# Attention and routed MoE on one core: z and v of the next batch split in another block, by another engine

## The chip, the cores and the metric

The kernel runs on one core of one Trainium2 chip. The metric is the device time of one execution in microseconds (us); the median of the runs is compared. PE is TensorE, DVE is VectorE, ACT is ScalarE, POOL is GpSimd, SP is SyncE, which issues most of the DMAs.

## What is computed

The reference, cut to its core: attention without softmax, a dense MLP, then a routed one.

```python
B, S, D = u.shape                      # 8, 3072, 256;  z is 8 x 3072 x 64
scores = np.matmul(z, z.transpose(0, 2, 1)) / S
attn = np.maximum(scores, 0.0) ** 2
x = (u * np.matmul(attn, v)).reshape(B * S, D)
h = x @ w_in                           # 256 x 2048
x = (h * np.clip(h + 3.0, 0.0, 6.0) / 6.0) @ w_out
e_idx = np.argmax(x @ w_gate, axis=1)  # 8 experts, the best one for each token
out = gate * sigmoid(x @ w_output_gate) * (relu(x @ w1[e]) @ w2[e])
```

## The kernel before

**Precision by splitting.** Each operand of a matmul is held as a high part (rounded by a cast to the matmul's type) and a low part (the operand less its high part), and three products take the place of one. So every tile of z and of v is split when it arrives: a cast on ACT gives the high part and a subtraction gives the low one.

**Blocks.** A batch has 6 chunks of 512 tokens, 48 chunks in all. `order` (lines 132 to 142) is a list of units written out in advance. A block ("A", q) has 24 attention units, a block ("M", q) has 16 units of the dense MLP, and ("E", t, p) are the experts' units at the end. From the third M block on, A and M take turns: A(q), then M(q - 1), then A(q + 1). The M block between the last A block of one batch and the first A block of the next is called the M block between two batches here. There are 7 of them, and 7 last A blocks whose batch has a next one.

**One step.** `run` (lines 747 to 759) goes through the units. In step n it issues the front of unit n + 3 (`stage1`: the matmuls into one of two PSUM banks "psa", then the activation on ACT and, in an M unit, `gt` on DVE, line 232, which frees the bank), the middle of unit n + 2 (`stage2`: the split into `hit` and `lot`), and the products of unit n (`back`). All other work is hung on a step by `when(step, fn)`. Its instructions stand in their engines' queues behind those of step - 1 and in front of those of the step named. Each engine takes its queue in order, since `manual_schedule` keeps the order of issue.

**What an engine does in one unit.** In an A unit ACT makes two activations (lines 220 and 221) and DVE a cast (line 240) and a subtraction (line 243). In an M unit ACT makes line 231 and the cast of line 242, DVE lines 232 and 243. Beside the units of an A block DVE also makes 32 products for the routing of an earlier chunk (`gate_dot`, line 431). The routing's small instructions (`route`, lines 373 to 411) follow in the last steps of the A block and the first of the M block, with the product with u (`mul_x`, line 277) and the scatter of rows from POOL's queue (line 420).

**z and v of the next batch.** `plan_chunk` (lines 683 to 689) hangs them on the last A block of a batch, whose first unit is s0. `load_z` (two DMAs on SP's queue) and `prep_z1` run for 6 tiles of z, `load_v` (one DMA) and `prep_v` for 12 pairs of v tiles. `prep_z1` (lines 159 to 176) makes two casts on ACT and one subtraction, for the first tile of a batch two. `prep_v` (lines 190 to 196) makes one cast on ACT and one subtraction. For every batch but the first the subtractions of z are POOL's (line 172); those of v always are (line 195). Raw tiles have two buffers each ("zraw" and "vraw"), so a third load waits until a first one was split. The high and low parts of v have 12 buffers (`NV`), as many as a batch needs, and the split z has 7.

Of the kernel before, what the change touches and what calls it, by code (L numbers as in the profile page):

```python
# [8 lines left out]
F32 = mybir.dt.float32  # L9
# [10 lines left out]
P = 128  # L20
# [7 lines left out]
def kernel(  # L28
# [14 lines left out]
    DQ = zT.shape[1]  # L43
# [24 lines left out]
    pe, act, dve, pool, sp = nc.tensor, nc.scalar, nc.vector, nc.gpsimd, nc.sync  # L68
# [76 lines left out]
    def when(step, fn, early=False):  # L145
        bg.setdefault((max(step, low[0]), not early), []).append(fn)

# [1 line left out]
    z1, z2, zraw = {}, {}, {}  # L149
    vh, vl, vraw = {}, {}, {}  # L150
    xu = {}
# [1 line left out]
    def load_z(key, b, t):  # L153
        zr = ap.tile([P, TC], F32, tag="zraw", name="zr", bufs=2)
        for h in range(2):
            sp.dma_start(out=zr[h * DQ:(h + 1) * DQ], in_=zT[b, :, t * TC:(t + 1) * TC])
        zraw[key] = zr

    def prep_z1(key, b, t, with_z2=False):
        zr = zraw.pop(key)  # L160
        a = ap.tile([P, TC], F32R, tag="z1", name="z1t", bufs=NZ + 1)
        if with_z2:
            w = ap.tile([P, TC], F32R, tag="z2", name="z2t", bufs=2)
            z2[b, t] = w
        else:
            w = ap.tile([P, TC], F32R, tag="zs", name="zst", bufs=1)
        act.copy(a[0:DQ], zr[0:DQ])
        if b or t:
            act.copy(w[DQ:P], zr[DQ:P])
        else:  # L170
            dve.tensor_copy(w[DQ:P], zr[DQ:P])
        eng = pool if b else dve
        eng.tensor_sub(a[DQ:P], zr[DQ:P], w[DQ:P].bitcast(F32))
        if with_z2:
            eng.tensor_sub(w[0:DQ], zr[0:DQ], a[0:DQ].bitcast(F32))
        z1[b, t] = a

    def prep_z2(key, b, t):
        zr = zraw.pop(key)
        w = ap.tile([P, TC], F32R, tag="z2", name="z2t", bufs=2)  # L180
        act.copy(w[DQ:P], zr[DQ:P])
        dve.tensor_sub(w[0:DQ], zr[0:DQ], z1[b, t][0:DQ].bitcast(F32))
        z2[b, t] = w

    def load_v(b, i):
        r = ap.tile([P, 2, D], F32, tag="vraw", name="vr", bufs=2)
        sp.dma_start(out=r, in_=v[b, 2 * i * P:2 * (i + 1) * P, :].rearrange("(a p) d -> p a d", p=P))
        vraw[b, i] = r

    def prep_v(b, i):  # L190
        r = vraw.pop((b, i))
        h = ap.tile([P, 2, D], F32R, tag="vh", name="vht", bufs=NV)
        l = ap.tile([P, 2, D], F32R, tag="vl", name="vlt", bufs=NV)
        act.copy(h, r)
        pool.tensor_sub(l, r, h.bitcast(F32))
        vh[b, i], vl[b, i] = h, l

    def load_u(q):
        b, c = divmod(q, NC)
        t = mp.tile([P, ND, TC], F32, tag="xu", name="xut", bufs=2)  # L200
        sp.dma_start(out=t, in_=uT[b, :, c * TC:(c + 1) * TC].rearrange("(d p) t -> p d t", p=P))
        xu[q] = t

# [1 line left out]
    tmp_t, hi_t, lo_t, o_t = {}, {}, {}, {}  # L205
    xh, xl = {}, {}

# [64 lines left out]
                mm(o[s], gh, wo[:, i].rearrange("p k d -> p (k d)"), i == 0, False)  # L272
                mm(o[s][:, :D], gl, wo[:, i, 0, :], False, i == NF - 1)

# [1 line left out]
    def mul_x(q, d):  # L276
        dve.tensor_mul(xu[q][:, d, :], xu[q][:, d, :], o_t[q][d][:, :TC])

    def split_x(q, d):
        if q in alt:  # L280
            if d == 0:
                alt[q] = pools["e"].tile([P, 2, ND, TC], F32R, tag="ws", name="xat", bufs=NPAIR + 2)
            h, l = (alt[q][:, k, d, :] for k in range(2))
        else:
            h = mp.tile([P, TC], F32R, tag="xph", name="xht", bufs=ND)
            l = mp.tile([P, TC], F32R, tag="xpl", name="xlt", bufs=ND)
        act.copy(h, xu[q][:, d, :])
        xh.setdefault(q, []).append(h)
        xl.setdefault(q, []).append(l)

    def split_xl(q, d):
        pool.tensor_sub(xl[q][d], xu[q][:, d, :], xh[q][d].bitcast(F32))

    def save_x(q):
        sp.dma_start(out=xsave[q], in_=xu.pop(q).rearrange("p d t -> p (d t)"))

    def reload_x(q):
        t = mp.tile([P, ND, TC], F32, tag="xu", name="xut", bufs=2)
        sp.dma_start(out=t, in_=xsave[q].rearrange("p (d t) -> p d t", d=ND))
        xu[q] = t  # L300

    alt = {NQ - 1: None, 1: None}

# [1 line left out]
    raw = {}  # L305

    def load_w(which, f):
# [45 lines left out]
        pool.tensor_sub(mf, mf, h.bitcast(F32))  # L353
        pool.tensor_add(l, mf, sc)

# [1 line left out]
    rt = {}  # L357

    def rtile(name, shape, dt=F32):
# [53 lines left out]
    def evacuate(q, s):  # L413
        o, row = o_t["x", q], row_of(q)
        act.activation(row[:, s, :D], o[s][:, :D], AF.Copy, scale=1.0 / 6.0)
        dve.scalar_tensor_tensor(row[:, s, :D], o[s][:, D:], 1.0 / 6.0, row[:, s, :D],  # L416
                                 op0=ALU.mult, op1=ALU.add)

    def scatter(q, s):
        pool.indirect_dma_start(  # L420
            out=xs_d,
            out_offset=bass.IndirectOffsetOnAxis(ap=rt["di", q][:, s:s + 1], axis=0),
            in_=row_of(q)[:, s, :],
            in_offset=None,
        )

    def gate_dot(q, k):
        s, e = divmod(k, E)
        if k == 0:
            rt["lg"] = rtile("lg", [P, NSUB, E])  # L430
        dve.tensor_tensor_reduce(junk, row_of(q)[:, s, :D], gbc[:, e, :], 1.0, 0.0, op0=ALU.mult, op1=ALU.add,  # L431
                                 accum_out=rt["lg"][:, s, e:e + 1])

# [1 line left out]
    small = {}  # L435

    def stile(name, w=E):
# [72 lines left out]
                           min_val=e * REG, max_val=e * REG + NT)  # L510
        sp.dma_start(out=xs_d[bass.ds(r, SLOT), :].rearrange("(a p) c -> p a c", p=P), in_=zrow)

# [1 line left out]
    rows, wraw, wreg, wnew, ws, ogw, gt = {}, {}, {}, {}, {}, {}, {}  # L514
    y_ps = []

# [122 lines left out]
        pools["row"] = pools["e"].tile([P, NSUB, RW], F32, name="row1")  # L639
        pool.memset(pools["row"][:, :, D + 2:RW], 0.0)  # L640

# [1 line left out]
    def plan_chunk(q):  # L643
        b, c = divmod(q, NC)
        s0, e0 = at["A", q, 0], at["A", q, NJ - 1]
        m0, m1 = at["M", q, 0], at["M", q, NF - 1]
        if q > 1:
            when(s0 + 4, lambda: load_u(q))
        if c > 0:
            when(s0 - 14, lambda: load_z(("2", q), b, c))  # L650
            when(s0 - 8, lambda: prep_z2(("2", q), b, c))
        for d in range(ND):
            when(e0 + 1 + 2 * d, lambda d=d: mul_x(q, d))
        if q < NSAVE:
            when(e0 + 5, lambda: save_x(q))
            when(m0 - NF - 8, lambda: reload_x(q))
        sx = m0 - NF + 4 if q < NSAVE or q == NQ - 1 else m0 - NJ + 2
        for d in range(ND):
            when(sx + 2 * d, lambda d=d: split_x(q, d))
            when(sx + 2 * d + 1, lambda d=d: split_xl(q, d))  # L660
        kind = order[m1 + 1][0]
        rate = {"A": 1.6, "M": 3.0 if q else 1.0, "E": 0.5}[kind]
        d0 = m1 + 2 if kind != "E" else m1 + 22
        for k in range(NSUB * E):
            when(d0 + int(k / rate), lambda k=k: gate_dot(q, k))
        n = d0 + int(NSUB * E / rate)
        for s in range(NSUB):
            when(m1 + 1 + (s if kind == "A" else 0), lambda s=s: evacuate(q, s))
        for st in range(1, 5):
            when(n + st - (st == 1), lambda st=st: route(q, st))  # L670
        sc = m1 + NJ + 2 if kind == "A" else n + 4
        if q < NSAVE:
            E0 = at["E", 0, 0]
            sc = max(E0 + 1, sc + (E0 + 1 - sc) % NPAIR)
        for st in range(NSUB):
            when(sc + (st * NPAIR if q < NSAVE else 0), lambda st=st: scatter(q, st))
        if q == 1:
            for st in range(4):
                when(n + 6 + st, lambda st=st: table2a(st))
            when(n + 11, lambda: tableb(1))  # L680
            for e in range(E):
                when(sc + NPAIR * (NSUB + e), lambda e=e: fill_tail(e))
        if c == NC - 1 and b + 1 < B:
            for t in range(NZ):
                when(s0 + 4 * t - 2, lambda t=t: load_z(("1", b + 1, t), b + 1, t))
                when(s0 + 4 * t + 2, lambda t=t: prep_z1(("1", b + 1, t), b + 1, t, t == 0))
            for i in range(NV):
                when(s0 + 2 * i - 2, lambda i=i: load_v(b + 1, i))
                when(s0 + 2 * i + 2, lambda i=i: prep_v(b + 1, i))

    for q in range(NQ):
        plan_chunk(q)
# [28 lines left out]
    load_v(0, 0)  # L721
    setup_consts()
    prep_z1(("1", 0, 0), 0, 0, True)
    prep_v(0, 0)
    load_z(("1", 0, 1), 0, 1)
    load_v(0, 1)
# [13 lines left out]
    front = {"A": stage1, "M": stage1, "E": e1}  # L740
    middle = {"A": stage2, "M": stage2, "E": lambda u: None}
    behind = {"A": back, "M": back, "E": e3}
# [68 lines left out]
```

## Time and profile before

| what | us |
|---|---|
| median of 3 runs | 5626.42 (5626.34 to 5627.16) |
| span of the profiled execution, first to last instruction | 5624.6 |
| what lies around that span, against the median | 1.8 |
| PE busy | 5533.8 (98%) |
| DVE busy | 4356.8 (77%) |
| ACT busy | 3446.1 (61%) |
| POOL busy | 1084.1 (19%) |

The page gives the profiled execution by its span; its own time outside the span is not listed, so the median stands in for it. Busy shares are means over stages, so this profile is read block by block: the start of a block is the start of its first matmul into "psa". In a timeline a row has the start, the duration and the instruction, with the idle time before it and what ended that in brackets. A group of instructions has count, busy time and mean duration, and behind the second bar the idle time in front of them. In a table of windows each engine has its busy time and, in brackets, its instructions, then the granted clock of PE as a share of 2.4 GHz, the DMA engines' busy share and GB/s.

### The profile page before, as it was taken

Reading aid. Unit: us, or ns where it says so; the run is one execution under the profiler, and the core shown is the slowest. Engines: PE = TensorE matmul, PEld = TensorE weight load, DVE = VectorE, ACT = ScalarE, POOL = GpSimd, SP = SyncE. Lnnn points to the kernel's source line nnn. Section 1 sums busy time; section 2 is a strip of 40 time slices with the busy share of each in tenths; the row PEclk is TensorE's granted clock in tenths of the full one; section 3 lists DMA queues with packets and bytes.
Section 4 is the critical chain, followed back from the end, with each engine's and each line's share of the span. In section 5 each row is a group of like instructions: output and inputs, shape, how many; then the busy total and the mean of one; then the engine's idle time right before and its main releaser. Section 6 shows DMA issues by size and latency. Waiting matters only on the chain.

```text
span 5624.6 us, 83062 instructions
## 1 busy us (share of the span) xinstructions
PE 5533.8 (98%) x28472; PEld 4644.1 (83%) x28472; DVE 4356.8 (77%) x9925; ACT 3446.1 (61%) x5870; POOL 1084.1 (19%) x915
## 2 busy tenths in 40 slices
PE   9999999999999999999999999999999999999999
PEld 6778887888788878887888788878888899999998
DVE  9877777767776777777776877686767888888887
ACT  7655565656565565556565656565555577777776
POOL 3220002000200020002000200020001144444443
PEclk9999999999999999999999999999999999999999
DMA  3110001000100010001000100010000122222243
GB/s 103 42 45 17 14 16 46 16 14 16 46 16 14 18 44 18 18 14 47 14 16 16 46 14 16 16 46 14 16 16 12 50 75 82 81 72 73 76 116 114
DMA packets 133151, 216.92 MB, mean 39 GB/s; under 512 B 16605, under 2 KB 85982, under 8 KB 132576
## 3 DMA queue, kind: packets, MB, share of 16 engines
q1 hardware_dynamic: 113888, 160.66, 9.9%
q0 software_dynamic: 18816, 50.75, 2.5%
q8 instruction: 225, 3.69, 0.3%
q14 instruction: 222, 1.82, 0.1%
HBM read 157.17 MB, written 55.22 MB: 38 GB/s over the span
## 4 chain that ended last, share of the span: by engine, by line
PE 88%; DVE 7%; issue 3%; ACT 1%; POOL 1%; DMA 0%; POOLq 0%; SPq 0%; ACTq 0%; DVEq 0%
PE psa L209 36%; PE psx L209 28%; PE pso L209 24%; DVE lot L243 2%; DVE hit L240 2%; DVE junk L431 1%; PE pso L574 1%; POOL out L625 0%; DVE wst L567 0%; ACT at L220 0%; DVE lot L597 0%; DVE r_cnt L394 0%; DVE cvt L323 0%; ACT gt L231 0%; DVE row L416 0%
## 5 line engine op out<-in xcount | busy, mean ns | idle before, releaser
L231 ACT ACTIVATE gt<-psa,three 128x512 f32<-128x512 f32 x768 | 528.8, 689 | 1147.4 <-PE psa L209 1076.2
L232 DVE SCALAR_TENSOR_TENSOR gt<-gt,psa 128x512 f32<-128x512 f32 x768 | 527.8, 687 | 878.2 <-ACT gt L231 877.9
L209 PE MATMUL psx<-wo,hit 128*128 128x512 f32 x3072 | 1112.5, 396 | 0.0
L209 PE MATMUL psa<-xht,win 128*128 128x512 f32 x2944 | 1039.5, 393 | 3.0 <-DVE gt L232 2.9
L220 ACT ACTIVATE at<-psa 128x512 f32<-128x512 f32 x1152 | 687.5, 597 | 552.9 <-PE psa L209 416.4
L243 DVE TENSOR_TENSOR lot<-at,hit 128x512 fp32r<-128x512 f32 x1152 | 882.9, 766 | 49.4 <-DVE hit L240 0.5
L209 PE MATMUL pso<-lot,vht 128*128 128x512 f32 x2208 | 891.7, 404 | 27.1 <-DVE lot L243 26.6
L209 PE MATMUL pso<-hit,vht 128*128 128x512 f32 x2208 | 883.3, 400 | 34.2 <-DVE hit L240 34.2
L209 PE MATMUL pso<-hit,vlt 128*128 128x512 f32 x2208 | 878.3, 398 | 0.0
L209 PE MATMUL psx<-wo,lot 128*128 128x256 f32 x3072 | 860.3, 280 | 0.0
L221 ACT ACTIVATE at<-at 128x512 f32<-128x512 f32 x1152 | 729.1, 633 | 36.7
L431 DVE CUSTOM_DVE_ANT_0 junk<-row,gbc 128x256 f32<-128x256 f32 x1536 | 714.2, 465 | 19.7
L209 PEld LDWEIGHTS psx<-wo,hit 128*128 128x128 f32 x3072 | 577.0, 188 | 136.2
L209 PEld LDWEIGHTS psa<-xht,win 128*128 128x128 f32 x2944 | 552.9, 188 | 134.5 <-DVE gt L232 5.6
L209 PE MATMUL psa<-xht,wst 128*128 128x256 f32 x3200 | 649.3, 284 | 1.9 <-DVE wst L567 1.3
L209 PEld LDWEIGHTS psx<-wo,lot 128*128 128x128 f32 x3072 | 579.6, 189 | 30.6
L243 DVE TENSOR_TENSOR lot<-gt,hit 128x512 fp32r<-128x512 f32 x768 | 527.6, 687 | 73.1 <-ACT hit L242 73.1
L209 PE MATMUL psa<-xlt,win 128*128 128x512 f32 x1472 | 580.1, 394 | 0.0
L209 PE MATMUL psx<-wst,hit 128*128 128x512 f32 x1600 | 577.1, 394 | 0.0
L567 DVE TENSOR_TENSOR wst<-w,wst 128x1024 fp32r<-128x1024 f32 x400 | 572.2, 1431 | 0.0
L240 DVE CAST hit<-at 128x512 fp32r<-128x512 f32 x1152 | 566.8, 492 | 2.4 <-ACT at L221 2.2
L420 POOL DMA_INDIRECT xs_d<-row,r_di x192 | 189.6, 988 | 1929.5 <-DVE row L411 1634.3
(154 smaller groups left out, 9251.5 us busy)
## 6 DMA issues: line engine op xcount, KB each, us to landing
w<-in_wcat SPq DMA_DIRECT2D x64, 512.0 KB
x<-xs_d SPq DMA_DIRECT2D x100, 260.0 KB
vr<-in_v SPq DMA_DIRECT2D x96, 256.0 KB
xut<-in_uT SPq DMA_DIRECT2D x48, 512.0 KB
zr<-in_zT SPq DMA_DIRECT2D x176, 128.0 KB
ogt<-in_w_ogT SPq DMA_DIRECT2D x100, 128.0 KB
wraw<-in_w_in SPq DMA_DIRECT2D x16, 256.0 KB
wraw<-in_w_out SPq DMA_DIRECT2D x16, 256.0 KB
```

The costliest lines, as they stand in the source:

```text
L209: pe.matmul(o, l, r, start=start, stop=stop)
L220: act.activation(t, ps, AF.Relu, scale=1.0 / S)
L221: act.activation(t, t, AF.Square)
L231: act.activation(t, ps, AF.Relu, bias=three)
L232: dve.scalar_tensor_tensor(t, t, 6.0, ps, op0=ALU.min, op1=ALU.mult)
L240: dve.tensor_copy(h, t)
L243: dve.tensor_sub(l, t, h.bitcast(F32))
L420: pool.indirect_dma_start(out=xs_d, out_offset=bass.IndirectOffsetOnAxis(ap=rt["di", q][:, s:s + 1], axis=0), in_=row_of(q)[:, s, :], in_o ...
L431: dve.tensor_tensor_reduce(junk, row_of(q)[:, s, :D], gbc[:, e, :], 1.0, 0.0, op0=ALU.mult, op1=ALU.add, accum_out=rt["lg"][:, s, e:e + 1])
L567: dve.tensor_sub(w[:, :, 1, :], wraw[p], w[:, :, 0, :].bitcast(F32))
L574: pe.transpose(o[:, d, a * P:(a + 1) * P], x[:, a, d * P:(d + 1) * P], ident)
```

## The change

All subtractions of z and v for batches after the first go to DVE, and the steps they are hung on move behind e0, the last unit of the last A block. The changed lines that only remove comments are left out.

```diff
-        eng = pool if b else dve
-        eng.tensor_sub(a[DQ:P], zr[DQ:P], w[DQ:P].bitcast(F32))
+        dve.tensor_sub(a[DQ:P], zr[DQ:P], w[DQ:P].bitcast(F32))
         if with_z2:
-            eng.tensor_sub(w[0:DQ], zr[0:DQ], a[0:DQ].bitcast(F32))
+            dve.tensor_sub(w[0:DQ], zr[0:DQ], a[0:DQ].bitcast(F32))
...
         act.copy(h, r)
-        pool.tensor_sub(l, r, h.bitcast(F32))
+        (dve if b else pool).tensor_sub(l, r, h.bitcast(F32))
...
         if c == NC - 1 and b + 1 < B:
             for t in range(NZ):
-                when(s0 + 4 * t - 2, lambda t=t: load_z(("1", b + 1, t), b + 1, t))
-                when(s0 + 4 * t + 2, lambda t=t: prep_z1(("1", b + 1, t), b + 1, t, t == 0))
+                at_z = e0 + 1 + (5 * t) // 2
+                when(at_z - 4, lambda t=t: load_z(("1", b + 1, t), b + 1, t))
+                when(at_z, lambda t=t: prep_z1(("1", b + 1, t), b + 1, t, t == 0))
             for i in range(NV):
-                when(s0 + 2 * i - 2, lambda i=i: load_v(b + 1, i))
-                when(s0 + 2 * i + 2, lambda i=i: prep_v(b + 1, i))
+                at_v = e0 + 2 + (6 * i) // 5
+                when(at_v - 3, lambda i=i: load_v(b + 1, i))
+                when(at_v, lambda i=i: prep_v(b + 1, i))
```

The M block between two batches has the units e0 + 1 to e0 + 16. The splits of z stand at steps e0 + 1, 3, 6, 8, 11 and 13, those of v at e0 + 2, 3, 4, 5, 6, 8, 9, 10, 11, 12, 14 and 15.

## Rows read from the trace of the kernel before

**Rows 1.** The page, part 1: busy time of each engine

```profile
PE 5533.8 (98%) x28472; PEld 4644.1 (83%) x28472; DVE 4356.8 (77%) x9925; ACT 3446.1 (61%) x5870; POOL 1084.1 (19%) x915
```

**Rows 2.** Windows of the 7 last A blocks: first, last, sum

```profile
339.84:398.70 58.86, 48.75 (x200) 36.76 (x199) 55.22 (x113) 42.37 (x75) 26.60 (x18) 0.97 0.23 70
...
3648.63:3706.85 58.22, 51.07 (x201) 38.88 (x200) 54.60 (x112) 42.35 (x75) 26.31 (x18) 0.91 0.21 64
sum 408.80, PE 348.91 PEld 265.21 DVE 383.41 ACT 296.78 POOL 184.67; mean PE 49.84 PEld 37.89 DVE 54.77 ACT 42.40 POOL 26.38
```

**Rows 3.** Windows of an M block and an A block inside a batch

```profile
488.42:533.10 44.68, 44.68 (x222) 37.26 (x221) 24.61 (x52) 19.47 (x34) 3.87 (x4) 1.00 0.03 12
533.10:577.95 44.85, 44.85 (x201) 36.18 (x199) 41.13 (x121) 32.00 (x56) 2.72 (x2) 1.00 0.07 19
```

**Rows 4.** Windows of the 7 M blocks between batches, each with the next A

```profile
398.70:488.42 89.72, 89.72 (x419) 73.43 (x418) 69.21 (x179) 53.20 (x93) 11.53 (x9) 1.00 0.08 26
...
sum 631.68, PE 628.60 PEld 514.05 DVE 487.70 ACT 372.66 POOL 81.71; mean PE 89.80 PEld 73.44 DVE 69.67 ACT 53.24 POOL 11.67
```

**Rows 5.** Groups of instructions in the first of these last A blocks, 339.84 to 398.70

```profile
L243 DVE TENSOR_TENSOR lot<-at,hit 128x512 fp32r<-128x512 f32 x22 | 20.1, 914 | 1.0
...
L195 POOL TENSOR_TENSOR vlt<-vr,vht 128x512 fp32r<-128x512 f32 x10 | 13.9, 1388 | 4.9 <-PE psa L209 4.1 <-ACT vht L194 0.6
```

**Rows 6.** Timeline of POOL in that block

```profile
351.31 1.62 POOL L173 TENSOR_TENSOR z1t<-zr,z2t 64x512 fp32r<-64x512 f32 x1 [33.62 <-ACT z2t L169]
353.01 1.37 POOL L175 TENSOR_TENSOR z2t<-zr,z1t 64x512 fp32r<-64x512 f32 x1
```

**Rows 7.** Timeline of DVE in the same stretch

```profile
351.69 1.53 DVE L431 CUSTOM_DVE_ANT_0 junk<-row,gbc 128x256 f32<-128x256 f32 x1
...
353.62 1.04 DVE L240 CAST hit<-at 128x512 fp32r<-128x512 f32 x1
```

**Rows 8.** Timeline of PE in that block, its longest wait

```profile
360.67 0.50 PE L209 MATMUL pso<-hit,vht 128*128 128x512 f32 x1 [2.36 <-DVE hit L240]
```

**Rows 9.** Window right behind that wait

```profile
361.50:365.00 3.50, 2.65 (x6) 2.15 (x7) 3.47 (x6) 1.23 (x2) 1.86 (x2) 0.56 0.23 57
```

**Rows 10.** Groups over the whole span: costs of the moved work

```profile
L194 ACT CAST vht<-vr 128x512 fp32r<-128x512 f32 x96 | 59.1, 616 | 6.1 <-PE pso L209 3.9 <-DMA vr<-in_v 1.0
...
L167 ACT CAST z1t<-zr 64x512 fp32r<-64x512 f32 x48 | 29.1, 607 | 1.4 <-DMA zr<-in_zT 1.4
...
L173 DVE TENSOR_TENSOR z1t<-zr,zst 64x512 fp32r<-64x512 f32 x5 | 3.4, 689 | 1.7 <-ACT zst L169 1.6
```

**Rows 11.** Groups of the M block inside a batch, 488.42 to 533.10

```profile
L231 ACT ACTIVATE gt<-psa,three 128x512 f32<-128x512 f32 x16 | 11.0, 689 | 25.2 <-PE psa L209 23.4 <-issue 1.8
L232 DVE SCALAR_TENSOR_TENSOR gt<-gt,psa 128x512 f32<-128x512 f32 x16 | 11.0, 688 | 19.6 <-ACT gt L231 19.6
```

**Rows 12.** Timeline of DVE at the start of that M block

```profile
498.25 0.68 DVE L277 TENSOR_TENSOR xut<-xut,pso 128x512 f32<-128x512 f32 x1
499.18 0.69 DVE L232 SCALAR_TENSOR_TENSOR gt<-gt,psa 128x512 f32<-128x512 f32 x1 [0.24 <-ACT gt L231]
```

**Rows 13.** Timeline of PE there: the front that reuses this PSUM bank

```profile
502.44 0.40 PE L209 MATMUL psa<-xht,win 128*128 128x512 f32 x1
```

**Rows 14.** Timeline of PE in an M block between two batches

```profile
961.22 0.50 PE L209 MATMUL psa<-xht,win 128*128 128x512 f32 x1 [0.71 <-DVE gt L232]
```

**Rows 15.** Timeline of DVE there

```profile
960.48 0.68 DVE L232 SCALAR_TENSOR_TENSOR gt<-gt,psa 128x512 f32<-128x512 f32 x1
...
964.96 0.68 DVE L243 TENSOR_TENSOR lot<-gt,hit 128x512 fp32r<-128x512 f32 x1
```

**Rows 16.** Timeline of POOL there, a scatter

```profile
964.73 0.99 POOL L420 DMA_INDIRECT xs_d<-row,r_di  x1 [5.19 <-DVE row L411]
```

**Rows 17.** Timeline of SP's queue in the first last A block

```profile
355.83 0.37 SPq L187 DMA_DIRECT2D vr<-in_v  x1
```

**Rows 18.** Timeline of ACT there: the cast of what that DMA loads

```profile
358.91 0.62 ACT L194 CAST vht<-vr 128x512 fp32r<-128x512 f32 x1
```

## The prediction

> **What bounds the kernel now.** First the page: PE is busy for 5533.8 us of 5624.6 [rows 1]. That looks like a kernel with 91 us to win at most, and it hides where they lie, so I read it block by block. A block inside a batch has no idle PE at all: 44.68 us of 44.68 in an M block, 44.85 of 44.85 in an A block [rows 3]. The last A block of a batch does the same matmuls and takes some 58 to 59 us. The seven sum to 408.80 us where 7 x 44.85 = 313.95 would do: 94.85 us too many, of which PE idles 408.80 - 348.91 = 59.9 us [rows 2, 3]. The other 34.96 us are matmuls that run longer: behind the block's longest wait, 2.36 us, the granted clock was 0.56 of full speed for 3.5 us [rows 8, 9], so partly at the lower level of 1.2 GHz, and each block's share is 0.91 to 0.97. The M block behind it, with the A block that follows, is a little late too: 631.68 us for seven, against 7 x (44.68 + 44.85) = 626.71, so 4.97 us [rows 3, 4].
>
> Why is it the last A block? The waits end on DVE's `hit` and `lot`. DVE is busy for 383.41 us in these seven blocks, where 7 x 41.13 = 287.91 is usual [rows 2, 3]: 95.5 us more, though no instruction of z or v runs on it there. POOL runs 26.4 us of subtractions a block in place of 2.7. The timelines side by side show what happens. While POOL's z subtraction runs from 351.31 to 352.93, a routing product of DVE that begins at 351.69 takes 1.53 us and so ends only behind POOL. With POOL's next one, from 353.01 to 354.38, a cast takes 1.04 us [rows 6, 7]. The mean of `lot` in this block is 914 ns [rows 5], where one with no POOL subtraction beside it takes 0.68 us [rows 15]. So each POOL subtraction, 1.39 us for v [rows 5], holds up one DVE instruction for about a microsecond, 95.5 us over 7 x 19 subtractions being 0.72 us each. An A unit lasts 44.85 / 24 = 1.87 us and DVE works for 41.13 / 24 = 1.71 of them, so there is no room for it.
>
> **What is removed.** From the last A blocks (and the first steps behind them, where the last two or three run) go 7 x 19 POOL subtractions, 7 x 24 ACT casts and 7 x 24 DMAs on SP's queue. What remains in such a block is what the A block of [rows 3] has, `mul_x` and the routing included, and that one has no idle PE. So I take back the whole 94.85 us. The clock's share is in that sum, since without the waits nothing lowers it: in the plain blocks it is 1.00 [rows 3]. Below: nothing more can come, since PE is already busy for all of a plain block. The 4.97 us behind it come from the same pile: DVE enters the M block late, and `gt` at 960.48 holds PE for 0.71 us [rows 14, 15]. I take these back as well.
>
> **What is added.** To the M block between two batches go 7 subtractions of z (two for the first tile) and 12 of v on DVE at 0.69 us each [rows 10], 13.1 us, and 24 casts on ACT at 0.61 [rows 10], 14.7 us. Neither runs on PE. In a plain M block DVE is busy for 24.61 of 44.68 us and ACT for 19.47 [rows 3]. After the change they come to 37.7 and 34.2, both still under 44.68. By the unit, 2.79 us long, ACT idles 25.2 / 16 = 1.58 us and DVE 19.6 / 16 = 1.2 [rows 11].
>
> Is there room at the worst step? That is e0 + 1 to e0 + 3, where the routing's end and `mul_x` stand too. There `gt` starts at 499.18 after 0.24 us of idle time, and ends at 499.87. PE wants the bank that it frees at 502.44, so it can be 2.57 us late for nothing [rows 12, 13]. The two z subtractions of step e0 + 1 stand ahead of it on DVE, behind the `mul_x` of 498.25. That ends at 498.93, and 2 x 0.69 us more make 500.31, so `gt` is 1.1 us late. At step e0 + 3 a z, a v and a `mul_x` come together, 2.1 us against a mean idle time of 1.2, and `gt` is 0.9 us late. On ACT the fullest steps hold three casts, 1.85 us against 1.58, so line 231 is 0.3 us late. Behind a late `gt` stand `lot` (read two units later) and the next splits; nobody waits for these within the slack of 2.57. So I cost the added work at 0. The other end: if none of it were hidden, DVE's 13.1 us in seven blocks would be 92 us on the path. The nearest row is the plain M block with its 20 us of idle DVE, so I stay at 0, and keep for the range two waits like the 0.71 of [rows 14] in each block, 2 x 7 x 0.71 = 9.9 us.
>
> **The queues.** POOL's queue loses its subtractions; the M block has only scatters on it. One of 0.99 us begins at 964.73, and a DVE subtraction with both inputs in SBUF begins 0.23 us later and takes its plain 0.68 us [rows 15, 16]. So scatters cost the added subtractions nothing. The Trainium skill, on the page SBUF — State Buffer, section Who interferes with whom, has a rule against this change: a DVE instruction with two SBUF inputs contends with a GpSimd instruction that reads SBUF, and one of the two then blocks fully; a scatter reads its row numbers there. By that rule the four scatters of each block could hold DVE, and with all of that on the path the sum would be the 5554.3 of rival (e); the row above disagrees.
>
> On SP's queue a load of v is asked for three steps ahead, yet the splits come 1.2 steps apart and there are two raw buffers. So the load of pair i waits on SP for the subtraction of pair i - 2, and the loads behind it, of z too, wait with it. From that subtraction's end to the cast of pair i there are two steps, 5.6 us, less about 1.5 us for the cast and the subtraction: 4.1 us, and some 2.7 us early in the block, where DVE is late. One such load was issued at 355.83 and its cast at 358.91 waited for nothing [rows 17, 18], so landing takes at most 3.1 us. A cast up to 1 us late still fits into ACT's idle time. Cost 0.
>
> **The sum.** 94.85 + 4.97 = 99.8 us. The traced execution has a span of 5624.6 us, the median is 5626.4; the 1.8 us around the span stay. So 5626.4 - 99.8 = 5526.6 us, 1.8% less.
>
> **The rivals.** (a) DVE's pile at the start of the M block costs PE time. For it: DVE idles only 0.24 us at 499.18 [rows 12], and there is a row where a late `gt` held PE [rows 14]. Against it: that one came later than 2.57 us of slack allow, mine is 1.1 late. One wait of 0.71 in each block gives 5531.6, two 5536.5. (b) The A block doesn't recover wholly, because ACT's casts and the loads were part of its trouble elsewhere and come back with the next A. Against it: the plain A block [rows 3]. Half the gain kept would give 5576.5. (c) Slower than before: the loads of v land late. The cast then holds up ACT's queue, line 231 behind it, `gt`, and PE. The place is the 12 loads of each M block; it decides from a landing time of about 4.1 + 1 + 2.57 = 7.7 us, beyond which each load costs PE the excess. To eat 99.8 us over 84 loads it takes 1.2 us each, a landing of 8.9 us; at 9.5 us the time would be 5526.6 + 84 x 1.8 = 5678. The 3.1 us of [rows 17, 18] speak against it. (d) The change doesn't do what it says, because the queue's wait pushes the splits out of the M block: no gain, 5626. Against it: the last split stands at step e0 + 15, and its first reader, the product of the next A block's 23rd unit, comes over 20 steps later. (e) Scatters block DVE: each of four scatters in a block holds one subtraction for up to 0.99 us, which costs 0 to 28 us, so 5526.6 to 5554.3; the one pair in [rows 15, 16] says no. This is what the rule of the Trainium skill's page SBUF — State Buffer above would come to.
>
> **How the numbers follow.** Forecast 0.81, (a) 0.11, (b) 0.03, (c) 0.02, (d) 0.01, (e) 0.02. Measurement tells 0.2% from no change, 11 us. All but (c) and (d) are faster by more than that: faster 0.97, same 0.01, slower 0.02. The range runs from 5524 to 5538. Below the forecast there is only the runs' spread, 0.8 us, and the rounding of some twenty block times, for which 2.6 us are enough. Above it stand two waits in each M block, 5536.5, and the same spread. It holds the forecast and (a), 0.92.
>
> **What would show it.** Right: every A block at 44.8 to 45.0 us with PE idle 0; the M blocks between batches at 44.7; DVE busy in the last A block near 41 us and in the M block behind it near 38; POOL busy there for some 3 us; the clock at 1.00 in every block; `lot` near 690 ns in all of them. Wrong: PE waits for `gt` in the first steps of the M block (a), ACT's cast `vht` waiting for the DMA of line 187 (c), or DVE instructions of 1 us and more beside a scatter (e).

## The result and the profile after

The changed kernel takes 5527.57 us (median of 4 runs, 5527.39 to 5528.0), the kernel before 5626.53 us (4 runs). The ratio is 0.9824, with a 95% interval of 0.9811 to 0.9837: 99.0 us less, where 99.8 was predicted, and a time 1.0 us above the predicted 5526.6. Line numbers behind the changed code are one lower after (`lot` is line 242 now, `gt` 231); in the experiments they shift with each edit.

Part 1 of the page after, busy time of each engine, answers to [rows 1]:

```profile
PE 5498.1 (99%) x28472; PEld 4632.5 (84%) x28472; DVE 4315.2 (78%) x10058; ACT 3448.2 (62%) x5870; POOL 885.8 (16%) x782
```

133 instructions went from POOL (915 to 782) to DVE (9925 to 10058), which is 7 x 19. DVE took them in and yet is busy for 41.6 us less. That is the first thing to see: the 133 subtractions cost DVE more while POOL made them than they do now that DVE makes them itself.

Windows of the 7 last A blocks after (columns as in [rows 2], which they answer to):

```profile
339.94:384.80 44.86, 44.86 (x200) 36.18 (x199) 41.15 (x121) 32.00 (x56) 2.71 (x2) 1.00 0.00 1
...
sum 314.05, PE 314.05 PEld 253.28 DVE 288.09 ACT 224.00 POOL 18.98; mean PE 44.86 PEld 36.18 DVE 41.16 ACT 32.00 POOL 2.71
```

Windows of the 7 M blocks between batches, each with the A block that follows (these answer to [rows 4]), and of the first such M block alone:

```profile
384.80:474.35 89.55, 89.55 (x420) 73.44 (x418) 77.05 (x189) 64.00 (x112) 7.26 (x6) 1.00 0.22 66
...
sum 626.83, PE 626.83 PEld 514.05 DVE 539.36 ACT 447.87 POOL 50.28; mean PE 89.55 PEld 73.44 DVE 77.05 ACT 63.98 POOL 7.18
...
384.80:429.49 44.69, 44.69 (x222) 37.26 (x220) 34.76 (x68) 31.05 (x56) 4.54 (x4) 1.00 0.37 108
```

In every sum PE's busy time equals the length of the windows, so PE never idles, and the granted clock is 1.00. The last A blocks gave back 408.80 - 314.05 = 94.75 us and the pairs behind them 631.68 - 626.83 = 4.85, together 99.6. The span fell by 98.5 us (5624.6 to 5526.1), so 1.1 us came back in parts that the change doesn't touch: 0.4 in one A block inside a batch (3384.56 to 3429.86, 45.3 us long, where PE waits 0.2 us for `lot`) and 0.4 behind the last of these pairs. Why is not known.

Groups of instructions of that M block after, where the added work now is (compare [rows 10, 11]):

```profile
L231 DVE SCALAR_TENSOR_TENSOR gt<-gt,psa 128x512 f32<-128x512 f32 x16 | 11.0, 686 | 7.6 <-ACT gt L230 7.5
L242 DVE TENSOR_TENSOR lot<-gt,hit 128x512 fp32r<-128x512 f32 x14 | 9.6, 684 | 0.0
L194 DVE TENSOR_TENSOR vlt<-vr,vht 128x512 fp32r<-128x512 f32 x10 | 6.9, 689 | 0.3 <-ACT vht L193 0.2
L193 ACT CAST vht<-vr 128x512 fp32r<-128x512 f32 x11 | 6.8, 621 | 0.5 <-DMA vr<-in_v 0.4
L419 POOL DMA_INDIRECT xs_d<-row,r_di x4 | 4.5, 1134 | 51.2 <-DVE row L410 43.6 <-DMA xs_d<-row,r_di 7.6
```

The idle time in front of `gt` fell from 19.6 us to 7.6: that is the room that the subtractions went into. No DVE operation got longer, not beside the four scatters either.

DVE's timeline at the start of the block, the step that the prediction worked out as the worst:

```profile
395.36 0.69 DVE L172 TENSOR_TENSOR z1t<-zr,z2t 64x512 fp32r<-64x512 f32 x1
396.08 0.68 DVE L174 TENSOR_TENSOR z2t<-zr,z1t 64x512 fp32r<-64x512 f32 x1
396.69 0.68 DVE L231 SCALAR_TENSOR_TENSOR gt<-gt,psa 128x512 f32<-128x512 f32 x1
```

In the plain M block `gt` starts 10.76 us behind the block's start (499.18 - 488.42); here it is 396.69 - 384.80 = 11.89, so 1.1 us late. PE doesn't wait for it.

ACT's timeline, the one place of this block where the loads of v are late by more than a trace of time:

```profile
404.77 0.62 ACT L193 CAST vht<-vr 128x512 fp32r<-128x512 f32 x1 [0.36 <-DMA vr<-in_v]
405.99 0.69 ACT L230 ACTIVATE gt<-psa,three 128x512 f32<-128x512 f32 x1 [0.60 <-PE psa L208]
```

The cast waits 0.36 us for its DMA, and the next activation still comes early enough to wait for PE. Over 205 to 4146 us, which holds all seven blocks, such casts wait 11 times, 5.5 us in all and 0.9 at most; in the whole stretch behind 205 us PE waits for `gt` once, for 0.8 us. That wait stands behind 4146 us, where the kernel before has one of 0.9 us as well.

### The profile page after: what moved, and what is told of

It reads as the page before. It is cut to its first block, busy times and chain, and to the rows that moved or that the text cites. A ratio compares the mean times of both kernels' runs of the same rounds, so it can differ in the third digit from the quotient of the medians.

```text
span 5526.1 us, 82916 instructions
## 1 busy us (share of the span) xinstructions
PE 5498.1 (99%) x28472; PEld 4632.5 (84%) x28472; DVE 4315.2 (78%) x10058; ACT 3448.2 (62%) x5870; POOL 885.8 (16%) x782
## 3 DMA queue, kind: packets, MB, share of 16 engines
HBM read 157.17 MB, written 55.22 MB: 38 GB/s over the span
## 5 line engine op out<-in xcount | busy, mean ns | idle before, releaser
L242 DVE TENSOR_TENSOR lot<-at,hit 128x512 fp32r<-128x512 f32 x1152 | 859.7, 746 | 49.0 <-DVE hit L239 0.5
L430 DVE CUSTOM_DVE_ANT_0 junk<-row,gbc 128x256 f32<-128x256 f32 x1536 | 653.8, 426 | 19.8
L239 DVE CAST hit<-at 128x512 fp32r<-128x512 f32 x1152 | 537.5, 467 | 2.3 <-ACT at L220 2.2
```

The costliest lines, as they stand in the source:

```text
L239: dve.tensor_copy(h, t)
L242: dve.tensor_sub(l, t, h.bitcast(F32))
```

## The experiments

The rows above agree with the prediction; they don't show that its reasons are the right ones. The questions were: is it the place or the engine that carries the gain; does POOL's subtraction hold DVE; and how far is the change from the waits that the rivals named? Each kernel was compared with the kernel before on the same chip (5626.15 to 5626.84 us). Times are of one run unless runs are named.

### The place alone

The steps of the change, with POOL making the subtractions as before:

```diff
-        dve.tensor_sub(a[DQ:P], zr[DQ:P], w[DQ:P].bitcast(F32))
+        eng = pool if b else dve
+        eng.tensor_sub(a[DQ:P], zr[DQ:P], w[DQ:P].bitcast(F32))
...
-        (dve if b else pool).tensor_sub(l, r, h.bitcast(F32))
+        pool.tensor_sub(l, r, h.bitcast(F32))
```

> The steps move behind e0 as in the change, but POOL makes the subtractions. Theory (the place decides: the last A block has no room on VectorE, the M block has): 19 POOL subtractions hold up one VectorE instruction each, 0.7 us, 13.7 us in a block with 20 us of idle VectorE, so 5527 to 5535 us, PE idle under 1 us in the M blocks. Rival (the engine decides: POOL's subtractions hurt wherever they stand): over 5590.

Measured: 5595.0 us, some 60 us above the theory's range and where the rival put it. The last A blocks recovered, but the M blocks between two batches took 53.3 to 54.6 us. The trace shows why. First the window of the first such M block, then the timeline of POOL, ACT, DVE and PE inside it:

```profile
384.89:439.08 54.19, 47.31 (x222) 39.12 (x220) 27.77 (x51) 30.92 (x56) 26.57 (x21) 0.91 0.26 77
```

```profile
399.00 0.99 POOL L420 DMA_INDIRECT xs_d<-row,r_di  x1 [1.64 <-DVE row L411]
...
407.19 0.96 POOL L420 DMA_INDIRECT xs_d<-row,r_di  x1 [1.73 <-DMA xs_d<-row,r_di]
408.18 1.27 POOL L195 TENSOR_TENSOR vlt<-vr,vht 128x512 fp32r<-128x512 f32 x1
...
412.34 0.62 ACT L194 CAST vht<-vr 128x512 fp32r<-128x512 f32 x1 [10.52 <-DMA vr<-in_v]
...
413.58 0.69 DVE L232 SCALAR_TENSOR_TENSOR gt<-gt,psa 128x512 f32<-128x512 f32 x1 [10.95 <-ACT gt L231]
...
414.32 0.80 PE L209 MATMUL psa<-xht,win 128*128 128x512 f32 x1 [6.88 <-DVE gt L232]
```

Read it from the top. Four scatters stand on POOL's queue, and each waits some 1.8 us for the DMA of the one before; so the queue is taken from 399.00 to 408.15. The subtraction of v behind them starts at 408.18. Until it ends, its raw buffer isn't free, so the next load isn't issued, ACT's cast waits 10.52 us, line 231 stands behind the cast, `gt` behind that, and PE idles for 6.88 us. With the wait the granted clock of the block falls to 0.91. This is the chain of rival (c), started by POOL's queue and not by a slow DMA. POOL is busy for only 26.57 of 54.19 us: not its work is the trouble but its place in a queue with waits. So the time lies in the rival's range, but for another reason than the rival gave.

### The engine alone

The changed subtractions at the steps of the kernel before (in the last A block):

```diff
-                at_z = e0 + 1 + (5 * t) // 2
-                when(at_z - 4, lambda t=t: load_z(("1", b + 1, t), b + 1, t))
-                when(at_z, lambda t=t: prep_z1(("1", b + 1, t), b + 1, t, t == 0))
+                when(s0 + 4 * t - 2, lambda t=t: load_z(("1", b + 1, t), b + 1, t))
+                when(s0 + 4 * t + 2, lambda t=t: prep_z1(("1", b + 1, t), b + 1, t, t == 0))
...
```

> The steps stay in the last A block, but VectorE makes the subtractions. Theory (no room on VectorE in the last A block, whoever fills it): 19 x 0.6 to 0.69 us more against some 4 to 7 us that are really free, so 5 to 10 us lost in each block, 5562 to 5598 us. Rival (only the sharing between POOL and VectorE costs): 5527 to 5532.

Measured: 5579.68 us, inside the expectation. Window of the first last A block:

```profile
339.84:392.17 52.33, 49.09 (x200) 35.28 (x199) 47.98 (x128) 42.50 (x76) 2.73 (x2) 1.00 0.25 76
```

DVE has more work than the 44.86 us of a plain block can hold (47.98), and the block takes 7.5 us too long, 52.3 us over seven. So the engine alone is worth 47.1 us, the place alone 31.8 us, and both together 99.0, more than the two added up (78.9).

### Without the low part of v

The kernel before, with v's 12 subtractions left out for batches 1 to 7; the product of the low part of v then uses its high part again, so this part of the computation is changed.

```diff
+        if b:
+            vh[b, i], vl[b, i] = h, h
+            return
         pool.tensor_sub(l, r, h.bitcast(F32))
```

> The kernel before without the 12 subtractions of v per batch (the low part of v is left out for batches 1 to 7, the high part stands in for it); ACT's casts, the loads and z's subtractions stay in the last A block. Theory (POOL's subtractions make the loss): 7 of 19 are left, so about 7/19 of 14 us a block, 5 us, 5540 to 5575 us. Rival (ACT's casts and the loads in the last A block make it): 5600 to 5626.

Measured: 5555.15 us, inside the expectation. Window of the first last A block:

```profile
339.94:388.77 48.83, 46.38 (x200) 35.65 (x199) 45.19 (x113) 42.08 (x75) 12.92 (x8) 1.00 0.27 81
```

Taking 12 instructions away from POOL takes 10.0 us of busy time away from DVE (55.22 in [rows 2] to 45.19), on which nothing was changed. With the casts and the loads still there (ACT 42.08), 10 of the 14 us are gone. So the casts and loads were not the main trouble of the block.

### POOL's subtraction against POOL's fill

Two kernels put unused POOL work into the last A blocks of the changed kernel, at the steps s0 + 2 to s0 + 20: the first a 128x512 subtraction of two SBUF tiles, the second three fills of the same tile. A one-column copy of ACT and a one-column addition of POOL ahead of each set its time.

```diff
+        act.copy(bal[:, i:i + 1], three)
+        pool.tensor_scalar_add(o[:, 0, 0:1], bal[:, i:i + 1], 0.0)
+        pool.tensor_sub(o, gbc[:, 0:2, :], gbc[:, 2:4, :])
...
+            for i in range(19):
+                when(s0 + 2 + i, lambda i=i: ballast(i))
```

In the second kernel the last line of `ballast` is `for _ in range(3): pool.memset(o, 0.0)`.

> The changed kernel with 19 subtractions of 128x512 on POOL in each last A block whose result nobody reads, one a step from s0 + 2 on. No other engine's data depend on them. Theory (POOL's mere running holds VectorE): the last A blocks go back to 56 to 60 us, 5605 to 5630 us. Rival (the loss came from waits on z's and v's tiles and buffers): 5527 to 5532.

> As the ballast of 19 subtractions in each last A block, but POOL fills the same tile three times a step instead (it writes SBUF and reads nothing of it, beside a one-column instruction that keeps the pace). Theory A (whatever POOL runs on SBUF holds VectorE's instructions): last A blocks of 55 to 63 us as with the subtractions, 5600 to 5645 us. Theory B (POOL's reading is what holds VectorE's two-input instructions and products): 45 to 49 us, 5528 to 5556 us.

Measured: 5645.27 us with the subtractions, beyond the expected range, and 5529.05 us with the fills, at the low end of 5528 to 5556. Window and groups of the first last A block, with subtractions:

```profile
339.81:400.55 60.74, 51.46 (x200) 36.38 (x199) 57.23 (x108) 33.59 (x74) 36.96 (x40) 0.97 0.00 1
...
L651 POOL TENSOR_TENSOR bo<-gbc 128x512 f32<-128x512 f32 x19 | 27.9, 1468 | 1.6
...
L243 DVE TENSOR_TENSOR lot<-at,hit 128x512 fp32r<-128x512 f32 x21 | 20.3, 965 | 0.9
...
L240 DVE CAST hit<-at 128x512 fp32r<-128x512 f32 x21 | 16.1, 766 | 0.0
```

with fills:

```profile
339.80:385.05 45.25, 45.05 (x200) 36.20 (x199) 41.67 (x113) 33.56 (x74) 31.50 (x58) 1.00 0.00 1
...
L652 POOL MEMSET bo<- 128x512 f32 x42 | 24.4, 581 | 2.4
...
L243 DVE TENSOR_TENSOR lot<-at,hit 128x512 fp32r<-128x512 f32 x22 | 15.2, 693 | 1.0
...
L240 DVE CAST hit<-at 128x512 fp32r<-128x512 f32 x22 | 12.7, 579 | 0.0
```

and in the changed kernel itself, with neither:

```profile
L242 DVE TENSOR_TENSOR lot<-at,hit 128x512 fp32r<-128x512 f32 x23 | 17.1, 741 | 1.0
...
L239 DVE CAST hit<-at 128x512 fp32r<-128x512 f32 x23 | 10.5, 455 | 0.0
```

The block took 60.7 us with the first and 45.3 with the second, though POOL was busy for 37.0 and 31.5 us, not far from each other. So it isn't POOL being busy, and not its queue, that stretched the last A blocks of the kernel before: it is the subtraction that reads two tiles, here with no data from anything in the block. (Whether an instruction that reads one tile would do the same was not tried.) `lot` is at 965 ns beside it, near the 914 of [rows 5], and 693 beside the fills. The cast, which reads one tile, is held as well, 766 ns for 455. The subtractions cost DVE 57.23 - 41.15 = 16.1 us in this block. Some of DVE's work (13 of 121 instructions) runs only in the M block behind it and makes DVE busy for 37.92 us there in place of 34.76. Together that is 19.2 us, 1.0 us for each subtraction, where the prediction worked out 0.72 from the last A blocks alone.

### The place alone, with the scatters asked for later

The first experiment's kernel, with the four scatters of these M blocks 11 steps later:

```diff
-        sc = m1 + NJ + 2 if kind == "A" else n + 4
+        sc = m1 + NJ + (13 if q % NC == NC - 3 else 2) if kind == "A" else n + 4
```

> The steps moved and POOL subtracting, as in the run that cost 5595.0 us, with the four scatters of the M block between two batches asked for 11 steps later, behind most splits. Theory (there the splits stood behind the scatters in POOL's queue, so the raw buffers came free late, the load landed late and ScalarE's cast held up the rest): without them ahead the M blocks take 44.7 to 46.5 us, 5527 to 5541 us. Rival (POOL's holding of VectorE costs in the M block too): 5575 to 5595 us.

Measured: 5555.75 us. Every M block between batches is back at 44.69 us, as the theory had it; the time is not, since the A blocks behind them now take 47.8 to 50.8 us. Windows of the first M block and the A block behind it, then POOL's timeline:

```profile
384.69:429.37 44.68, 44.68 (x221) 37.25 (x220) 29.86 (x51) 30.95 (x56) 23.43 (x17) 1.00 0.29 84
429.37:477.20 47.83, 45.54 (x200) 36.18 (x199) 44.12 (x121) 33.05 (x58) 10.52 (x8) 1.00 0.14 45
```

```profile
438.13 1.01 POOL L420 DMA_INDIRECT xs_d<-row,r_di  x1 [1.92 <-DMA xs_d<-row,r_di]
440.89 1.57 POOL L173 TENSOR_TENSOR z1t<-zr,zst 64x512 fp32r<-64x512 f32 x1 [1.75 <-PE pso L209]
442.54 2.78 POOL L195 TENSOR_TENSOR vlt<-vr,vht 128x512 fp32r<-128x512 f32 x2
```

Only the scatters moved, and the 10 us wait of the M block is gone: that settles its cause. The last three splits stand behind the scatters again, run in the next A block, and cost DVE 3 us there (44.12 for 41.15). In the M block POOL is busy for 23.43 us beside DVE, and that costs nothing: POOL's subtractions hold DVE there too (`lot` is at 1112 ns in the mean), but DVE has room. The scatters can't be put behind the last split either, it seems: the routing of the next chunk writes the same rows, so scatters that late would make it wait (argued from the program, not tried).

### How much more DVE could take

Each subtraction of v made twice, or three times, on DVE, same data and place:

```diff
+        for _ in range(2 if b else 0):
+            dve.tensor_sub(l, r, h.bitcast(F32))
```

> The changed kernel with each of v's subtractions made twice on VectorE for batches 1 to 7 (same result): 12 x 0.6 to 0.69 = 7.2 to 8.3 us more in each M block between batches, where VectorE is busy for 34.8 of 44.7 us. Theory (hidden while VectorE has room): still 44.7 to 46 us a block, 5527 to 5536 us. Rival (the added work already sits on the path, so that more of it costs its own length): 5578 to 5586 us.

> The changed kernel, with each subtraction of v for batches 1 to 7 made three times on DVE (same data, same place). Theory (the move is free only while the M block and the A block behind it have idle DVE time): twice 12 x 0.69 = 16.6 us more in each of 7 blocks. With v made twice, M block and next A block already had 84.4 us of DVE in 90.1; with 8.3 us more that is 92.7 against the 89.5 that PE needs, so at least 3.2 us late in each and up to some 7: 5555 to 5580 us. Rival (DVE's queue only runs late, and later idle time takes all of it up): under 5540 us.

Measured: 5533.42 us twice, and 5595.48 us three times (4 runs, ratio to before 0.9945, 0.9928 to 0.9962), above the expected range. Windows of the first M block and the A block behind it, made twice:

```profile
384.80:429.29 44.49, 44.49 (x220) 37.06 (x219) 40.41 (x76) 31.03 (x54) 5.21 (x4) 1.00 0.32 94
429.29:474.91 45.62, 45.40 (x200) 36.11 (x199) 44.03 (x125) 32.97 (x58) 2.99 (x2) 1.00 0.12 37
```

and three times:

```profile
384.48:435.11 50.63, 46.69 (x221) 37.11 (x220) 46.23 (x86) 30.95 (x55) 4.06 (x4) 1.00 0.26 79
435.11:483.80 48.69, 46.72 (x198) 35.97 (x199) 46.97 (x129) 33.43 (x59) 3.53 (x2) 1.00 0.13 39
```

Of 8.3 us more on DVE, 5.7 show in the M block (40.41 for 34.76), which stays at its length, and 1.8 in the A block behind it (44.03 for the 42.28 of the changed kernel), which pays 0.8 us. The rest is the overlap of records that follow each other closely. With 16.6 us more the two need 93.2 us of DVE, close to the 92.7 expected (PE needs 89.5), but take 99.3, not 93 to 97. Who PE waited for in them (us in total, times, longest):

```profile
PE psa L210 <- DVE gt L233: 3.9, 7, 1.1
```

The subtractions stand in front of `gt`, for which PE waits 3.9 us of its 5.9 us of idle time, and DVE idles for 6 us in other steps. So a sum of busy time is too kind a test once the room is gone. The 13.1 us of the change could grow by 8.3, more than half, for 0.8 us in each pair of blocks.

### One raw buffer of v

```diff
-        r = ap.tile([P, 2, D], F32, tag="vraw", name="vr", bufs=2)
+        r = ap.tile([P, 2, D], F32, tag="vraw", name="vr", bufs=1)
```

> The changed kernel with one raw buffer for v in place of two, so that a load of v starts only when the split before it is done (batch 0 at the start of the kernel too). Theory (loads land in 2.3 to 3.1 us, two buffers give just enough lead, ScalarE's cast waits in front of the MLP's activation when they don't): each load is 1 to 1.8 us late against 1 us of free ScalarE time a step, so 45 to 53 us in the M blocks between batches, 5530 to 5590 us. Rival (the lead is ample, loads never matter): M blocks of 44.7 us, and only the start is longer, 5527 to 5535 us.

Measured: 5626.94 us, the time of the kernel before, and above the theory's 5530 to 5590: the M blocks take 52.0 to 54.0 us, the A blocks behind them 49.0 to 49.9, and the start of the kernel, whose v goes through the same buffer, 11.8 us more. ACT's timeline in the first M block:

```profile
413.58 0.62 ACT L193 CAST vht<-vr 128x512 fp32r<-128x512 f32 x1 [1.75 <-DMA vr<-in_v]
...
417.61 0.62 ACT L193 CAST vht<-vr 128x512 fp32r<-128x512 f32 x1 [2.31 <-DMA vr<-in_v]
```

A load that ACT waits for takes 2.6 to 3.0 us in this block, from its issue or from the end of the subtraction that frees the buffer to the cast; the one load of [rows 17, 18] took at most 3.1. With one buffer most of it lies on ACT's queue in front of line 230: the casts that wait do so for 1.4 to 2.6 us here. As much as the change gains hangs on the second buffer, 11.8 us of it in the start.

### Two tries for a better version

In the first 205 us of the changed kernel, where the weights are prepared, DVE is busy for 192 and PE idles some 14 us. One kernel gives a third of the casts there to ACT, the other moves the subtractions of the first batch's v from POOL to DVE as well:

```diff
-        if u[0] == "A":
+        if u[0] == "A" and not (u[1] < 4 and u[2] % 3 == 0):
             dve.tensor_copy(h, t)
         else:
             act.copy(h, t)
```

```diff
-        (dve if b else pool).tensor_sub(l, r, h.bitcast(F32))
+        dve.tensor_sub(l, r, h.bitcast(F32))
```

> A try for a better version: the changed kernel, with the cast of every third attention unit of the first four chunks made by ACT (0.61 us) and not by DVE (0.42 us). In the first 205 us DVE is busy for 192 and ACT for 150, and PE idles some 14 us there. Theory: DVE is what the start waits for, so 32 casts less on it, 13.4 us, give back part of the idle time: 5519 to 5527 us. Rival: ACT's own activations come later by its added 19.5 us and PE waits for them in place of DVE: 5527 to 5532 us.

> The changed kernel, with v of the first batch subtracted on DVE too. In the start POOL's 12 subtractions of v run beside a busy DVE. Theory (a POOL subtraction holds up DVE for about 0.7 us, as long as DVE would take for it): 12 x 0.69 = 8.3 us more work on DVE against 12 x 0.72 = 8.6 us less held up, so 5524 to 5531 us, no change. Rival: the start is bound by DVE's own work and POOL's subtractions are hidden in its idle time, then 8 us slower: 5533 to 5537 us.

Measured: 5549.52 us for the casts on ACT (4 runs), slower than both expectations. Waits in the first 227 us (who waited for whom, us in total, times, longest):

```profile
DVE lot L242 <- ACT hit L241: 51.7, 31, 3.8
...
ACT cvt L323 <- DVE cvt L322: 29.9, 28, 1.6
...
PE psa L208 <- ACT at L219: 8.1, 19, 0.9
```

and the second of these in the changed kernel, from 50 to 205 us:

```profile
ACT cvt L323 <- DVE cvt L322: 30.3, 28, 1.6
```

ACT waited for DVE's part of a weight conversion before this edit as well. New is the first wait: `lot` on DVE for a cast that stands in ACT's queue, 51.7 us of DVE's time. So the two engines wait for each other in turn. DVE's load up to the first M block fell from 192.4 to 164.4 us and the time rose by 22 us. In this kernel the order of two queues costs more than the load that was taken away; what bounds the start of the changed kernel isn't settled by it.

With the first batch's v on DVE: 5525.60 us (4 runs, 5525.25 to 5526.04; ratio to before 0.9821, 0.9804 to 0.9837), inside the expectation. Against its own runs of before it gains 100.6 us, the change 99.0. The intervals of the two ratios overlap, but the ranges of the times don't (the change took 5527.39 to 5528.0), and the traces show 1.3 us of the 1.6 in the start: the first M block begins at 204.04 us in place of 205.38. Window of the first 50 us, changed kernel, then this one:

```profile
0.00:50.00 50.00, 43.80 (x173) 33.20 (x174) 41.44 (x55) 42.17 (x73) 18.97 (x31) 1.00 0.47 142
```

```profile
0.00:50.00 50.00, 43.27 (x175) 33.62 (x176) 38.07 (x68) 42.67 (x73) 2.40 (x19) 1.00 0.48 142
```

DVE makes 13 instructions more and is busy for 3.4 us less.

## Why the prediction was right

**What bounds the kernel.** Shown. That POOL's subtraction holds up DVE was read from two pairs of rows and a mean; the subtraction against the fill shows it apart from everything else in the block, and leaving out v's subtractions shows it in the kernel before itself. The size was put too low. The 0.72 us come from the last A blocks alone, and part of the work that DVE couldn't do there ran in the M block behind. Over the last A blocks and the pairs behind them DVE was busy for 383.41 + 487.70 = 871.11 us before and for 288.09 + 539.36 = 827.45 after. The 827.45 hold the 133 subtractions, of 0.61 (from one start to the next) to 0.69 us each, so POOL's cost DVE some 125 to 135 us, 0.9 to 1.0 us each, as in the kernel with unused subtractions. The predicted time was not worked out from this term.

**What is removed.** 94.85 us predicted for the last A blocks, 94.75 measured; 4.97 for the pairs behind them, 4.85 measured. Taking the plain A block as the floor was right to a tenth of a microsecond because the block became the same block: 41.15 us of DVE for 41.13, 32.00 of ACT for 32.00. One thing was said too widely: `lot` was foreseen near 690 ns in all blocks, and its mean in this A block is 741, in the plain one before as well. The reason is what is left of the mechanism: POOL still makes two subtractions of `xlt` there, and one `lot` takes 1.82 us beside the second. How the 34.96 us of longer matmuls divide between the lower clock and other causes isn't shown: with the engine alone changed, the last A block has 49.09 us of matmuls for 44.86 at a granted clock of 1.00, so matmuls beside waits ran longer there without a lower clock.

**What is added.** Cost 0, as predicted. `gt` 1.1 us late in the worst step, as worked out, against 2.57 of slack, and 0.9 late behind the pile of step e0 + 3, as worked out too (402.03 - 384.80 = 17.23 us behind the block's start for 16.33 in the plain block). DVE's busy time in the block was put at 37.7 and came to 34.76, ACT's at 34.2 and came to 31.05. Three things lie between them: two of the 12 subtractions of v run behind the block's end, a subtraction of z for a later chunk that the plain block has (0.7 us) isn't in this one, and instructions that follow each other closely overlap in the records (the subtraction of 396.08 lasts 0.68 us, and `gt` starts 0.61 us after it began). For ACT one cast of v behind the block's end, one cast of z less and the overlap do the same. The margin is known now: 8.3 us more in each pair of blocks costs 5.9 us over the whole span, 16.6 us more costs 68.

**The queues.** SP's waits came as foreseen: casts up to 0.9 us late, taken up by ACT's idle time. The landing time, put at 3.1 us at most from one load, was 2.6 to 3.3 us where a cast behind 205 us waited for it; that is still far below the 7.7 of rival (c). Beside the four scatters DVE's subtractions keep 0.68 to 0.69 us; it is the scatter that got longer, 1134 ns in the mean for 966 in the plain M block. Over the whole changed kernel the 47 subtractions `lot` and `vlt` that overlap a scatter take 688 ns in the mean, those beside neither a scatter nor a two-input instruction of POOL 689. The rule of the Trainium skill that spoke against the change (SBUF — State Buffer, Who interferes with whom) did not decide it. By the wording of that section of the Trainium skill one of the two blocks, and here it was, if any, the one that nobody waits for. For subtraction and fill the same section of the Trainium skill says that POOL contends with a two-input DVE instruction only when it reads SBUF, and the two kernels agree: 965 ns for `lot` beside reads, 693 beside fills.

**The rivals.** (a) didn't come: one wait of 0.8 us for `gt` in the whole stretch. (c) was given 0.02 as a matter of landing time; its chain is real and came in two kernels without any slow load: when the splits stand behind scatters on POOL, and when there is one raw buffer. What the prediction didn't see is that the change of engine is needed in the new place for a second reason: it named POOL's queue as relieved, and didn't ask what would be queued there if the subtractions stayed. (d) and (e) are excluded by the windows and groups above.

**The sum.** 99.8 us predicted. By the spans it is 98.5: 0.2 us less from the two terms and 1.1 us in other blocks. By the medians it is 99.0; the 0.5 us between are of the size of the runs' spread.

## What to carry to other kernels

Ask of every helper engine not only how busy it is but what its instructions do to the engine that works beside it: here 133 subtractions given to the idle POOL cost the full DVE more than making them itself, 0.9 to 1.0 us each for 0.69. Work moved to another block wants three looks there: the idle time per step and not per block, the waits in the queue that it is put into, and the buffers that it holds while it waits. And look for the two halves of a change separately: here place and engine are worth 31.8 and 47.1 us alone and 99.0 together, because each alone runs into a wait that the other one removes.

## What the hardware showed that was not expected

A POOL that only fills tiles holds up DVE little even when busy for 31.5 of 45.25 us: two-input subtractions not at all (693 ns), casts some (579 ns for 455). The fills are shorter (0.58 us for 1.47), so a part of the difference may be due to length. Scatters on POOL's queue, which all write `xs_d`, follow each other only after a wait of some 1.8 us for the DMA of the one before (2.0 to 3.0 us in the first M block of the changed kernel), so four of them take the queue for 9 us with 4 us of work.
